# A transformer block on one core: the first transfers of x and of V's weights dealt anew between the two queues

## The chip, the core and the metric

The kernel runs on one core of one Trainium2 chip. The metric is device microseconds per execution: 555.67 us as the median of three runs (555.06 to 555.78).

## The reference, cut to what matters

One input x of 2048 rows by 576 columns (bfloat16) is normalised, then goes through a sliding-window attention and through a gated feed-forward, and the three are added.

```python
xn = _layernorm(x)                          # 2048 x 576, eps 1e-5
qkv = xn @ wqkv                             # 576 -> 3 * 576, 32 heads of 18
scores = einsum("bhqd,bhkd->bhqk", q, k) * 18 ** -0.5
scores = where(0 <= i - j < 256, scores, -1e9)
o = softmax(scores) @ v                     # heads joined again
attention = o @ wo                          # 576 -> 576
h = silu(xn @ w1) * (xn @ w3)               # 576 -> 4608
out = x + attention + h @ w2                # 4608 -> 576
```

## The kernel before, in words

The 2048 rows are worked in four chunks of 512 rows (`CH`), each of four tiles of 128 rows (`TB`). A chunk consists of the normalisation of its tiles, the projections to q, k and V, 36 units of the feed-forward's first half (`unit_pairs`, line 768, with the attention's steps dealt in between), and then the second half together with the output projection (`p2_mm`, line 839). The text speaks of tiles 1 to 4 of x as the change does; in the code they are t = 0 to 3.

Everything is written as a list of operations in program order (`add`). Each operation names the buffers that it reads (`r`), writes (`w`) or joins in writing (`j`), and `resolve` puts in the waits on semaphores. Every engine works through its own part of the list strictly in that order. So the order of lines is the order on each engine and on each of the two DMA queues, that of SyncE (q1 in the profile) and that of ScalarE (q10).

The change lies in the head, in what happens before the first feed-forward unit of the first chunk:

- SyncE requests tile 1 of x (`load_x`, line 306), V's weights for the contraction rows 0 to 511 in one transfer of 576 KB (line 897, buffer `wv`, key `wv`), the last 64 contraction rows in two small transfers (line 901, key `wvd`), and then the weights of q and k into the buffer `pt`: two transfers for the first half of the columns (line 927, key `wqk0`), two for the last 64 rows (line 931, key `wqkd`), two for the second half (`wqk1`). After these come the feed-forward weights (line 330), the first of which wait for tile 2's transposed values.
- ScalarE requests tiles 2, 3 and 4 of x and then loads its activation table (line 896).
- The normalisation of tile 1 is done by VectorE statistics (lines 396 and 399), a square root on ScalarE (line 369), a reciprocal (line 374) and the scaling (line 414). Tile 2's statistics are done on ScalarE (lines 387 and 390), those of tiles 3 and 4 on VectorE again. TensorE turns each tile (line 429), ScalarE copies the turned values to `xnT` (lines 442 and 448).
- V's projection (`proj_part`, line 500, kind "v") is done in two parts for each tile. In part 0 rows 0 to 63 of `wv` meet the first half of the columns and rows 64 to 127 the second half; in part 1 it is crossed. Each part therefore needs two quarters of `wv`. Part 1 ends with the 64 rows of `wvd`. The order on TensorE is: part 0 of tile 1, turning of tile 2, part 1 of tile 1, part 0 of tile 2, turning of tile 3, and so on.
- GpSimd regroups the weights of q and k from `pt` to `wp` (`deal`, line 952, eight copies, and one more copy on VectorE); the first of them needs `wqk0` and `wqkd`. The first part of q's projection (line 500, out of `xnT` and `wp`) needs the first two copies on GpSimd and the one on VectorE.
- `xn_swap` (line 463) then copies the halves of `xnT` crosswise to `xnS` by two transfers, behind the first six of the feed-forward weights. The first feed-forward unit reads `xnS` in its second half.

Of the kernel before, what the change touches and what calls it, by code (L numbers as in the profile page):

```python
# [44 lines left out]
class _Prog:  # L45
# [13 lines left out]
    def add(self, eng, fn, r=(), w=(), j=(), dma=None, after=()):  # L59
        deps = []  # L60
        for k in r:
            deps += self.bufs[k].writers
        for k in w:
            g = self.bufs.get(k)
            if g is not None:
                deps += g.ahead(eng)
        for k in j:
            g = self.bufs[k].before
            if g is not None:
                deps += g.ahead(eng)  # L70
        op = _Op(eng, fn, deps + list(after), dma)
        op.after = tuple(after)
        self.n[eng] += 1
        op.pos = self.n[eng]
        if dma is not None:
            self.dma_count[dma] = self.dma_count.get(dma, 0) + 16
            op.cnt = self.dma_count[dma]
        for k in r:
            self.bufs[k].readers.append(op)
        for k in w:  # L80
            self.bufs[k] = _Gen([op], self.bufs.get(k))
        for k in j:
            self.bufs[k].writers.append(op)
        for k in w:
            if self.bufs[k].before is not None:
                self.bufs[k].before.before = None
        self.ops.append(op)
        return op
# [76 lines left out]
def bass_parallel_sum__sliding_block__glu_gated_swiglu__prompt_kernel(  # L165
# [11 lines left out]
    D = A_x.shape[2]  # L177
# [11 lines left out]
    HD = D // 2  # L189
# [6 lines left out]
    add = P.add  # L196

    with ExitStack() as es:
# [17 lines left out]
        xnT = sb("xnT", [128, 2, 5, CH])  # L216
        xnS = sb("xnS", [128, 4, CH])
        wv = sb("wv", [128, 5, D])
# [83 lines left out]
        def load_x(t, eng="sp"):  # L302
            nonlocal xp_ctr
            s = xp_ctr % NXP
            xp_ctr += 1
            add(eng, lambda e: e.dma_start(xp[s][:], x2[t * 128:(t + 1) * 128, :]), w=[("xp", s)], dma=f"xp{s}")
            return s
# [167 lines left out]
        def proj_part(c, what, banks, part, behind=()):  # L475

            kind, i = what
            last = []
            early = kind == "v" and c == 0
            order = range(4 + part if kind == "v" else 5 - part)  # L480
            for n in order:
                for r in range(2):
                    x = r ^ part
                    kd, r0 = (4 if n == 4 else n), 64 * r
                    rows = slice(r0, r0 + 64)
                    out_ = PS[:, banks[x], :]
                    if kind == "q":
                        t = pair_of(c, i)[x]
                        st, mv = wp[rows, kd, t, :], xnT[rows, c % 2, kd, :]
                        keys = [("wp", t)] + xk(c)  # L490
                    elif kind == "8":
                        out_ = PS[:, banks[x], 0:CH // 2]
                        st, mv = wp[rows, kd, i, :], xnT[rows, c % 2, kd, x * (CH // 2):(x + 1) * (CH // 2)]
                        keys = [("wp", i)] + xk(c)
                    else:
                        out_ = PS[:, banks[x], 0:HD]
                        st, mv = xnT[rows, c % 2, kd, i * 128:(i + 1) * 128], wv[rows, kd, x * HD:(x + 1) * HD]
                        keys = ["wvd" if kd == 4 else "wv", (("xnTb" if kd // 2 else "xnTa"), i) if early and kd < 4 else ("xnT", c % 2, i)]
                    first = part == 0 and n == 0
                    op = add("pe", lambda e, out_=out_, st=st, mv=mv, n=n, r0=r0, first=first: e.matmul(  # L500
                        out_, st, mv, start=first, stop=(part == 1 and n == order[-1]), tile_position=(r0, 0)),
                        r=keys, after=behind if n == 0 else (), **{"w" if first else "j": [("ps", banks[x])]})
                    if n == order[-1]:
                        last.append(op)
            return last
# [384 lines left out]
                    p2_mm(ACC[half][tt] if turn is None or turn >= 0 else ACC[0][turn + 2], half, r, *args)  # L890


        xslot = {}
        for t in range(TB):
            xslot[t] = load_x(t, "act" if t else "sp")
        add("act", lambda e: e.preload_act_table_set("sqrt_and_others"))
        add("sp", lambda e: e.dma_start(
            wv[:, 0:4, :], A_wqkv[0:512, 2 * D:3 * D].rearrange("(kd p) f -> p kd f", p=128)),
            w=["wv"], dma="wv")
        for p in range(2):  # L900
            add("sp", lambda e, p=p: e.dma_start(
                wv[64 * p:64 * p + 64, 4, (1 - p) * HD:(2 - p) * HD],
# [21 lines left out]
        for h in range(2):  # L924
            for n in range(2):
# [3 lines left out]
                    dma=f"wqk{h}", **{"j" if n else "w": [f"wqk{h}"]})  # L929
# [119 lines left out]
        for c in range(NC):  # L1049
# [21 lines left out]
            early = [("h", n) for n in range(4 if c == 0 else 0, NHP)]  # L1071
# [111 lines left out]
            for u in range(NF):  # L1183
# [31 lines left out]
                if u in stat:  # L1215
                    t = (c + 1) * TB + stat[u]
# [4 lines left out]
                if u in apply:  # L1221
                    t = (c + 1) * TB + apply[u]
# [5 lines left out]
                if c == 0 and u == 13:  # L1228
                    for t in range(4):
# [24 lines left out]
            for item in p2_list(c):  # L1254
# [14 lines left out]
                elif n in (100, 120) and c + 2 < NC:  # L1269
                    t = (c + 2) * TB + (n == 120)  # L1270
# [34 lines left out]
```

## Time and profile before

| what | value |
|---|---|
| median of three runs | 555.67 us (555.06 to 555.78) |
| the profiled execution's own time | 555.25 us |
| its span, first to last instruction | 553.5 us |
| TensorE (PE) busy | 549.7 us, 99% of the span |
| VectorE / ScalarE / GpSimd busy | 57% / 47% / 38% |
| granted TensorE clock, mean | 1.000 |
| DMA queue of SyncE (q1) | 89138 packets, 62.80 MB |
| DMA queue of ScalarE (q10) | 38820 packets, 22.02 MB |

The profile comes from one execution, so sums are made against its own 555.25 us. The 1.75 us between it and the span lie around the program. The median of the runs is 0.42 us above the profiled execution. Times inside the trace are microseconds from the first instruction. A row of the timeline gives start, duration, engine, line, operation, names and count, and in brackets how long the engine was idle before it and what ended that. A row of the DMA issues gives the count, the size in KB (of 1024 bytes) and the time from issue to landing.

### The profile page before, as it was taken

How to read it: one execution, taken by the hardware profiler on the slowest of the kernel's cores; microseconds unless marked ns; L12 is line 12 of the kernel's file. 1: busy time of each engine (PE TensorE's matmuls, PEld its weight loads, DVE VectorE, ACT ScalarE, POOL GpSimd, SP SyncE). 2: the span in 40 equal slices, each digit the busy share in tenths (PEclk: the TensorE clock that was granted, in tenths of full speed). 3: DMA queues.
4: the chain of work that ended last, by engine and by line, in shares of the span. 5: the costliest groups of instructions: out<-in, count | busy, mean ns of one | idle time of the engine just before them, and what ended most of it. 6: DMA issues, size and time to landing. Idle time of an engine off the chain costs nothing.

```text
span 553.5 us, 18356 instructions
## 1 busy us (share of the span) xinstructions
PE 549.7 (99%) x8072; PEld 338.6 (61%) x8072; DVE 313.3 (57%) x587; ACT 259.3 (47%) x365; POOL 210.8 (38%) x380
## 2 busy tenths in 40 slices
PE   8999999999999999999999999999999999999998
PEld 5677544777555544477765454557776545445776
DVE  7476797710468886651056988655105567866311
ACT  7457776000288567700037857760005784775000
POOL 4324675400047456530005745643001553663100
DMA  9997799476577953756746885466673773541750
GB/s 246 204 199 173 199 202 229 129 202 181 141 144 145 188 134 92 186 141 194 185 111 140 173 157 146 124 143 164 183 181 85 139 172 102 152 117 44 194 151 23
DMA packets 128038, 86.00 MB, mean 155 GB/s; under 512 B 35702, under 2 KB 125646, under 8 KB 127958
## 3 DMA queue, kind: packets, MB, share of 16 engines
q1 hardware_dynamic: 89138, 62.80, 49.9%
q10 hardware_dynamic: 38820, 22.02, 15.7%
q8 instruction: 63, 1.03, 0.8%
q14 instruction: 17, 0.14, 0.1%
HBM read 71.29 MB, written 2.36 MB: 133 GB/s over the span
## 4 chain that ended last, share of the span: by engine, by line
PE 99%; DMA 1%; DVE 0%; issue 0%; ACT 0%
PE ps L768 51%; PE ps L839 29%; PE ps L500 10%; PE ps L630 6%; PE ps L698 3%; DMA xp<-in_A_x_dram 1%; PE ps L429 0%; DVE stats L396 0%; DVE xn L414 0%; ACT sd L369 0%; DVE ofin L861 0%; PE ps L915 0%; DVE mv L399 0%; DVE rstd L374 0%
## 5 line engine op out<-in xcount | busy, mean ns | idle before, releaser
L768 PE MATMUL ps<-xnT,w 64*128 64x512 bf16 x1400 | 186.4, 376 | 0.0
L768 PE MATMUL ps<-xnS,w 64*128 64x512 bf16 x1120 | 152.4, 376 | 0.0
L839 PE MATMUL ps<-w,hT 64*128 64x288 bf16 x2292 | 143.7, 282 | 0.0
L783 DVE SCALAR_TENSOR_TENSOR gs<-th,ps 128x512 bf16<-128x512 bf16 x144 | 97.9, 680 | 78.8 <-ACT th L777 78.0
L839 PEld LDWEIGHTS ps<-w,hT 64*128 64x128 bf16 x2292 | 112.3, 94 | 29.5 <-issue 0.2
L777 ACT ACTIVATE th<-ps 128x512 bf16<-128x512 f32 x144 | 85.6, 594 | 60.6 <-PE ps L768 59.7
L768 PEld LDWEIGHTS ps<-xnT,w 64*128 64x128 bf16 x1400 | 69.8, 94 | 61.6
L786 DVE SCALAR_TENSOR_TENSOR hT<-gs,ps 128x512 bf16<-128x512 bf16 x144 | 98.9, 687 | 5.0
L667 POOL TENSOR_TENSOR pt<-pt,mk 128x256 bf16<-128x256 bf16 (+1 forms) x143 | 85.6, 623 | 25.7 <-ACT pt L639 25.7
L639 ACT ACTIVATE pt<-ps 128x1024 bf16<-128x1024 f32 (+1 forms) x80 | 80.8, 1010 | 24.6 <-PE ps L630 24.1
L667 POOL TENSOR_TENSOR hT<-hT,mk 128x256 bf16<-128x256 bf16 (+1 forms) x52 | 30.3, 604 | 160.5 <-ACT hT L639 160.5
L768 PEld LDWEIGHTS ps<-xnS,w 64*128 64x128 bf16 x1120 | 55.6, 94 | 49.0
L513 ACT ACTIVATE stage<-ps 128x512 bf16<-128x512 f32 x16 | 9.6, 597 | 139.4 <-PE ps L500 139.4
L870 DVE TENSOR_TENSOR ofin<-ps,xp 128x288 bf16<-128x288 f32 x31 | 12.2, 451 | 98.5 <-PE ps L839 98.5
L630 PE MATMUL ps<-qv,kv 64*128 64x320 bf16 (+4 forms) x528 | 51.9, 260 | 0.0
L630 PEld LDWEIGHTS ps<-qv,kv 64*128 64x128 bf16 x528 | 26.8, 94 | 28.1 <-ACT pt L639 1.7
L500 PE MATMUL ps<-xnT,wp 64*128 64x512 bf16 (+1 forms) x360 | 38.4, 355 | 0.0
L731 DVE STREAM_TRANSPOSE od<-oq 128x256 bf16<-128x256 bf16 x64 | 25.4, 425 | 12.1 <-POOL oq L724 12.1
L639 ACT ACTIVATE hT<-ps 128x1024 bf16<-128x1024 f32 (+1 forms) x28 | 28.4, 1015 | 7.6 <-PE ps L630 7.4
L667 POOL TENSOR_TENSOR stage<-stage,mk 128x256 bf16<-128x256 bf16 (+1 forms) x44 | 24.8, 586 | 14.2 <-ACT stage L639 14.2
L639 ACT ACTIVATE stage<-ps 128x1024 bf16<-128x1024 f32 (+1 forms) x24 | 24.3, 1014 | 6.9 <-PE ps L630 6.8
L500 PEld LDWEIGHTS ps<-xnT,wp 64*128 64x128 bf16 x360 | 18.3, 94 | 14.5 <-ACT stage L513 0.2
(94 smaller groups left out, 395.9 us busy)
## 6 DMA issues: line engine op xcount, KB each, us to landing
w<-in_B_w_dram SPq DMA_DIRECT2D x210, 192.0 KB, 4.2
w<-in_B_w_dram ACTq DMA_DIRECT2D x70, 288.0 KB, 3.6
xp<-in_A_x_dram SPq DMA_DIRECT2D x29, 144.0 KB, 4.2
out_dram<-ofin SPq DMA_DIRECT2D x31, 72.0 KB, 1.7
xnS<-xnT SPq DMA_DIRECT2D x8, 256.0 KB, 4.7
oT<-od SPq DMA_DIRECT2D x56, 36.0 KB
pt<-in_A_wqkv_dram SPq DMA_DIRECT2D x4, 288.0 KB, 5.3
hT<-in_B_w_dram SPq DMA_DIRECT2D x6, 192.0 KB, 7.4
```

Of the source, the lines that this page charges most:

```text
L500: op = add("pe", lambda e, out_=out_, st=st, mv=mv, n=n, r0=r0, first=first: e.matmul(out_, st, mv, start=first, stop=(part == 1 and n == ...
L630: add("pe", lambda e, r0=r0, out_=out_, kb=kb, q0=q0, nb=nb: e.matmul(out_, kb4[r0:r0 + 64, g, kb + NV - NB, :] if kb < 0 else kv[r0:r0 + ...
L639: add("act", lambda e: e.activation(pt_slot(sl)[:, :, 0:w], PS[:, SC[0]:SC[1] + 1, 0:w], ACT.Exp, scale=scale), r=[("ps", b) for b in SC], ...
L667: add("pool", lambda e, vb=vb, mm=mm: e.tensor_tensor(vb, vb, mm, ALU.mult), r=(key if n == 0 else []) + ["mk"], **{"w" if n == 0 else "j" ...
L698: add("pe", lambda e, p=p, q=q, pr=pr, sl=sl, g=g, pos=pos, q0=q0, nb=nb, col=col, first=first, n=n: e.matmul(PS[32 * q:32 * q + VW, banks ...
L731: add("dve", lambda e: e.transpose(od[i][:, g % 2, c0:c0 + CH // 2], oq[:, c0:c0 + CH // 2]), r=["oq", "oq0"], **{"j" if half or g % 2 els ...
L768: op = add("pe", lambda e, n=n, r0=r0, r=r, k=k, src=src: e.matmul(PS[:, b0 + r, :], wt[r0:r0 + 64, k, fl * 128:(fl + 1) * 128], src, star ...
L777: add("act", lambda e: e.activation(th[i][:], PS[:, bg, :], ACT.Tanh, scale=0.5), r=[("ps", bg)], w=[("th", i)])
L783: add("dve", lambda e: e.scalar_tensor_tensor(out=gs[i][:], in0=th[i][:], scalar=1.0, in1=PS[:, bg, :], op0=ALU.add, op1=ALU.mult), r=[("t ...
L786: add("dve", lambda e: e.scalar_tensor_tensor(out=hT[:, u, :], in0=gs[i][:], scalar=0.5, in1=PS[:, bu, :], op0=ALU.mult, op1=ALU.mult), r= ...
L839: op = add("pe", lambda e: e.matmul(PS[:, bank, 0:w], stat, move, start=new, stop=False, skip_group_check=True, **tile), r=keys, after=hel ...
L870: add("dve", lambda e: e.tensor_tensor(ofin[:, o, :], PS[:, bank, 0:HD], xp[xs[n]][:, d0:d0 + HD], ALU.add), r=[("ps", bank), ("xp", xs[n] ...
```

## The change

V's weights for the rows 0 to 511 are requested in four quarters of 144 KB, each of 64 partitions, instead of in one transfer of 576 KB. The two quarters that part 0 multiplies (key `wv0`) are requested by ScalarE, behind tile 2 of x and ahead of its table load. The two that part 1 multiplies (key `wv1`) are requested by SyncE, behind tiles 1, 3 and 4 of x. ScalarE's list so holds three transfers ahead of the table load as before, with other contents. SyncE's holds three more than before ahead of `wvd`. V's matmuls wait for the key of their own part.

```diff
-                        keys = ["wvd" if kd == 4 else "wv", ...
+                        keys = ["wvd" if kd == 4 else f"wv{part}", ...
...
+        def load_wv(part, eng):
+            for p in range(2):
+                x = p ^ part
+                add(eng, lambda e, p=p, x=x: e.dma_start(
+                    wv[64 * p:64 * p + 64, 0:4, x * HD:(x + 1) * HD],
+                    A_wqkv[0:512, 2 * D + x * HD:2 * D + (x + 1) * HD].rearrange("(kd q p) f -> q p kd f", q=2, p=64)[p, :, :, :]),
+                    dma=f"wv{part}", **{"j" if p else "w": [f"wv{part}"]})
+
         xslot = {}
         for t in range(TB):
-            xslot[t] = load_x(t, "act" if t else "sp")
+            xslot[t] = load_x(t, "act" if t == 1 else "sp")
+        load_wv(0, "act")
         add("act", lambda e: e.preload_act_table_set("sqrt_and_others"))
-        add("sp", lambda e: e.dma_start(
-            wv[:, 0:4, :], A_wqkv[0:512, 2 * D:3 * D].rearrange("(kd p) f -> p kd f", p=128)),
-            w=["wv"], dma="wv")
+        load_wv(1, "sp")
```

More of the change, by code (lines that the diff above doesn't have):

```diff
@@ L497, in proj_part @@
                         st, mv = xnT[rows, c % 2, kd, i * 128:(i + 1) * 128], wv[rows, kd, x * HD:(x + 1) * HD]
-                        keys = ["wvd" if kd == 4 else "wv", (("xnTb" if kd // 2 else "xnTa"), i) if early and kd < 4 else ("xnT", c % 2, i)]
+                        keys = ["wvd" if kd == 4 else f"wv{part}", (("xnTb" if kd // 2 else "xnTa"), i) if early and kd < 4 else ("xnT", c % 2, i)]
                     first = part == 0 and n == 0
```

## The prediction, made before the changed kernel was run

> **What bounds the kernel now.** I read the page first: the busy time of the engines (part 1) and the chain that ended last (part 4).
>
> ```profile
> PE 549.7 (99%) x8072; PEld 338.6 (61%) x8072; DVE 313.3 (57%) x587; ACT 259.3 (47%) x365; POOL 210.8 (38%) x380
> ...
> PE 99%; DMA 1%; DVE 0%; issue 0%; ACT 0%
> ```
>
> TensorE is busy in 99% of the span, and the chain lies on it. The changed transfers all land in the first microseconds, so they can matter only as far as they shift the moment from which TensorE never waits again. The chain of waits for the first 24 us shows where that moment is (start, duration, what).
>
> ```profile
> 0.79 2.78 DMA xp<-in_A_x_dram
> 3.60 0.83 DVE stats L396 x2
> ...
> 4.69 0.30 ACT sd L369
> ...
> 5.22 0.42 DVE xn L414
> ...
> 6.49 0.67 PE ps L500 x8
> 7.16 0.21 PE ps L429 x10
> ...
> 10.46 10.64 PE ps L500 x118
> ```
>
> The head runs from tile 1's landing (0.79 + 2.78 = 3.57) over its normalisation to V's first part at 6.49. From 10.46 on TensorE feeds itself. V's weights do not appear in this chain, and of x only tile 1. So the question is not what the kernel gains when V's weights or tiles 3 and 4 come sooner, but whether a transfer that is hidden now comes out of its cover. For that I read the timeline, first the issues and ScalarE's start.
>
> ```profile
> 0.80 1.44 ACTq L306 DMA_DIRECT2D xp<-in_A_x_dram  x3
> 1.25 0.42 SPq L897 DMA_DIRECT2D wv<-in_A_wqkv_dram  x1
> 1.71 1.20 SPq L901 DMA_DIRECT2D wv<-in_A_wqkv_dram  x2
> 1.72 0.52 ACTq L306 DMA_DIRECT2D xp<-in_A_x_dram  x1
> 2.27 1.28 ACT L896 ACT_TABLE_LOAD   x1 [2.27 <-issue]
> 3.77 0.69 ACT L387 ACTIVATE hT<-xp 128x576 f32<-128x576 bf16 x1 [0.22 <-DMA xp<-in_A_x_dram]
> 4.69 0.60 SPq L931 DMA_DIRECT2D pt<-in_A_wqkv_dram  x1
> 5.33 1.14 SPq L927 DMA_DIRECT2D pt<-in_A_wqkv_dram  x2
> 8.25 4.90 SPq L330 DMA_DIRECT2D w<-in_B_w_dram  x6
> 13.84 0.60 SPq L463 DMA_DIRECT2D xnS<-xnT  x1
> ```
>
> Then those who use what is loaded, from the same view.
>
> ```profile
> 5.75 0.45 DVE L396 BATCH_NORM_STATS2 stats<-xp 128x6 f32<-128x288 bf16 x1
> 5.98 0.37 ACT L442 ACTIVATE xnT<-ps 128x256 bf16<-128x256 bf16 x1
> 7.21 0.48 PEld L500 LDWEIGHTS ps<-wv,xnT 64*128 64x128 bf16 x10
> 7.26 0.77 DVE L396 BATCH_NORM_STATS2 stats<-xp 128x6 f32<-128x288 bf16 x2
> 7.38 0.29 ACT L369 ACTIVATE sd<-mv,eps 128x1 f32<-128x1 f32 x1 [0.33 <-DVE mv L399]
> 8.00 0.11 PEld L500 LDWEIGHTS ps<-wv,xnT 64*128 64x128 bf16 x4 [0.30 <-ACT xnT L442]
> 10.13 0.84 POOL L952 COPY wp<-pt 128x360 f32<-128x360 f32 x2 [6.14 <-DMA pt<-in_A_wqkv_dram]
> 10.75 0.23 DVE L952 COPY wp<-pt 128x45 f32<-128x45 f32 x1
> 11.48 0.79 PEld L500 LDWEIGHTS ps<-xnT,wp 64*128 64x128 bf16 x10
> 21.52 0.81 PEld L768 LDWEIGHTS ps<-xnS,w 64*128 64x128 bf16 x8
> ```
>
> And the DMA issues, each asked for the moment of one issue, with the time from issue to landing. In this order: V's weights, tile 4 of x (the third on ScalarE's queue), the second of the small `wvd`, the second `wqkd`, the second half of `xnS`.
>
> ```profile
> wv<-in_A_wqkv_dram SPq DMA_DIRECT2D x1, 576.0 KB, 4.5
> ...
> xp<-in_A_x_dram ACTq DMA_DIRECT2D x1, 144.0 KB, 4.6
> ...
> wv<-in_A_wqkv_dram SPq DMA_DIRECT2D x1, 36.0 KB, 4.4
> ...
> pt<-in_A_wqkv_dram SPq DMA_DIRECT2D x1, 144.0 KB, 5.3
> ...
> xnS<-xnT SPq DMA_DIRECT2D x1, 256.0 KB, 6.8
> ```
>
> What is hidden, and by how much: V's weights land at 1.25 + 4.5 = 5.75, and V's first part also needs ScalarE's copy, which ends at 5.98 + 0.37 = 6.35: 0.60 us of cover. `wqkd` lands at 4.69 + 5.3 = 9.99 and GpSimd, idle for 6.14 us until then, starts its copies at 10.13. The two that q's first part needs end at 10.97, VectorE's at 10.98, and TensorE comes to q at 11.48: about 0.5 us of cover. The second half of `xnS` lands at 13.84 + 6.8 = 20.64 and is read at 21.52: 0.88 us. The shortest cover that lies behind all of the changed transfers is that of `wqkd`.
>
> How fast the transfers go is told by the windows (stretch, busy time by engine, clock, DMA share, GB/s).
>
> ```profile
> 4.00:5.00 1.00, 0.95 (x23) 0.65 (x19) 0.62 (x3) 0.86 (x4) 0.00 (x0) 1.00 1.09 389
> 6.00:7.40 1.40, 1.29 (x30) 0.96 (x30) 1.33 (x6) 1.06 (x6) 0.00 (x0) 1.00 1.15 312
> 8.00:8.50 0.50, 0.50 (x10) 0.23 (x8) 0.50 (x5) 0.41 (x2) 0.00 (x0) 1.00 0.92 161
> 11.50:16.00 4.50, 4.50 (x50) 2.61 (x48) 2.90 (x6) 2.91 (x7) 4.13 (x11) 1.00 1.13 221
> ```
>
> The share is about 1 in all four, so the DMA engines are the limit here, and not the issues. By the order of the queues the first stretch holds x and V's weights (128 partitions, pieces of 1152 bytes), the second the first half of the q and k weights (128 partitions, 576 bytes), the third `wqkd` (64 partitions, 2304 bytes), the fourth the feed-forward weights (64 partitions, 1024 bytes). Transfers to 64 partitions go at 161 to 221 GB/s, those to 128 at 312 to 389. The granted clock is 1.00 throughout.
>
> **The change part by part.**
>
> *Tiles 3 and 4 of x sooner.* VectorE takes up tile 3 at 5.75 and tile 4 at 7.26 with no wait for a transfer in the row, straight behind other work. Their earlier landing is worth nothing. Tile 1 stays the first on its queue and tile 2 on its own, beside the same neighbours; tile 1's landing would go into the sum one to one. I take 0, with bounds of 0.2 us either way: tile 2, first on the other queue, is taken up at 3.77 and tile 1 at 3.60.
>
> *ScalarE's list.* It issues three transfers as before. A quarter of V's weights has the shape nearest to `wvd` and `wqkd`, which cost 1.20 / 2 = 0.60 us an issue against 0.52 for tile 4. So the table load moves from 2.27 to about 0.80 + 0.41 + 2 x 0.64 = 2.5 and ends at 3.8. Line 387 starts at 3.77 because tile 2 lands then: at most some 0.05 us late. It is done by 4.6, before the square root of tile 1 at 4.69. Cost 0; if that cover of about 0.1 us is gone, the chain is late by the rest.
>
> *SyncE's list.* Two tiles of x (0.46 and 0.52 by ScalarE's rows) and one more issue for `wv1` (2 x 0.62 - 0.46) put everything behind about 1.75 us later: the second `wqkd` goes out at 6.4 instead of 4.69, the last `wqk1` ends at 5.33 + 1.14 + 1.75 = 8.2, and the feed-forward weights at 8.25 wait for tile 2's copy anyway. As transfers wait 4.4 to 5.3 us from issue to landing in a full queue, mostly behind others, later issues do not starve it. Cost 0.
>
> *V's first part on the ACT queue.* Its second quarter has the place that tile 4 has now, third on ScalarE's queue. That landed at 1.72 + 4.6 = 6.32, against the 6.35 of the copy. From below: 5.75, where V's weights land now, no wait. From above: 6.32 plus half of the 1.15 us extra worked out next, 6.9, a wait of 0.55. Behind this wait stand on TensorE the turning of tile 2, part 1 and all that follows. But the turned tile 2 is there at 7.37 and ScalarE first does the square root of tile 3, at 7.38 to 7.67, which waits for VectorE. So about 0.2 to 0.3 us of lateness costs nothing. I take a landing of 6.5, and 0.
>
> *The rate of V's 589,824 bytes.* At 389 GB/s they take 1.52 us. In pieces of 576 bytes over all partitions (312) they would take 1.89: 0.37 more. At the rate of the feed-forward weights (221) 2.67: 1.15 more. At that of `wqkd` (161) 3.66: 2.15 more. Half of the bytes (`wv0`) travel beside x tiles or beside the opposite half on the other queue, and half (`wv1`) mostly alone, first one half of the partitions and then the other. So I take the mean of the first two, 0.76. All that stands behind on SyncE's queue lands 0.76 later.
>
> [...]
>
> *Part 1.* `wvd` landed at about 2.33 + 4.4 = 6.73 as the last of the same bytes; 0.76 later is 7.49, and `wv1`, ahead of its 73,728 bytes (0.24 us at 312), 7.25. Part 1 starts at 7.21 and comes to `wvd` some 0.4 us later. Behind it TensorE waits 0.30 us for ScalarE at 8.00, which covers 0.04 us of lateness. Cost 0.
>
> *q's first part.* `wqkd` lands at 9.99 + 0.76 = 10.75, so GpSimd's two copies end at 11.73 and VectorE's at 11.0 to 11.1. TensorE, at q since 11.48, waits 0.25 us. From below 0 (0.37 stays under the cover of 0.5), from above 0.65 (1.15) or 1.65 (2.15). This wait and one in V do not add: who is late in V comes to q later.
>
> *Behind it.* `xnS` lands up to 0.76 later, within its 0.88, and TensorE comes 0.25 later itself. Cost 0.
>
> **Sum.** 555.25 + 0.25 = 555.50 for the profiled execution; the median is 0.42 above it: 555.92, say 555.9 us. 0.2% of 555.67 is 1.1 us, about what a measurement of this kernel can tell from no change.
>
> **The rivals.**
>
> *All hidden.* The quarters go at 312 GB/s because the two queues fill both halves of the partitions; `wqkd` lands at 10.36 and TensorE does not notice. For it: x beside them spreads over all partitions. Against: `wv1` is alone on its queue at the end. 555.7 us, within 0.2%.
>
> [...]
>
> *Slower by a slow `wqkd`.* The weights of q and k come out so late that GpSimd holds TensorE for longer than 1.1 us. It decides from 0.5 + 1.1 = 1.6 us of extra, which is V's weights below 188 GB/s. At the 161 of the third window q waits 1.65: 557.3 us. For it: `wqkd` reads the same matrix as V's weights, to 64 partitions too. Against: that is half a microsecond, in which two transfers change over.
>
> *Faster.* Tile 1 lands sooner because no 576 KB transfer starts behind it. It is worth 0.2 us by the bound above, 555.5; for 1.1 us the landing would have to be at 2.5, and nothing in the rows speaks for that.
>
> **How the numbers follow.** Forecast 0.60, all hidden 0.15, halves one after the other 0.11, slower 0.09, faster with the bound of 0.2 us or by what I do not see 0.05. The first two and the third in most runs lie within 1.1 us. Slower by over 0.2%: 0.09 and a third of the 0.11, with a little for the unnamed: 0.14. Faster by over 0.2%: 0.04. Same: 0.82. The range goes from 555.1, tile 1 sooner with the scatter of the runs (555.06 to 555.78), to 557.0, which takes in the halves one after the other (556.3, or 556.7 with that scatter) and leaves out the upper half of the slower case.
>
> **What would show it.** In the profile after: line 387 at 3.75 to 3.85; V's first part at 6.4 to 6.6; GpSimd's first copy at 10.5 to 11.3 instead of 10.13; the weight load of q's first part behind an idle time ended by GpSimd, at 11.6 to 12.1; a lower rate at 5 to 7 us; the distance from there to the end unchanged. I am wrong if line 387 or tile 1 moves by more than 0.2 us, if V's first part starts after 6.8, or if TensorE waits for `xnS` or a feed-forward weight at 20 to 40 us.

## The result: 0.33% slower, outside the range

| | median of 19 runs | ratio to before, 95% interval |
|---|---|---|
| before | 555.54 us | |
| changed | 557.52 us | 1.0033 (1.0021 to 1.0044) |
| changed, a second series (first experiment) | 556.93 us against 555.48 | 1.0023 (1.0013 to 1.0033) |

Predicted were 555.9 us, 555.1 to 557.0, and no difference that can be measured. The kernel became slower by 1.3 to 1.8 us.

The execution of the changed kernel that was profiled in the first series had a granted TensorE clock of 0.65 from 4.9 us on (0.656 on average) and took 827.17 us, so it is not in the ratio and its trace is not read for times. The same kernel was profiled again in the first experiment, at a clock of 1.000, and every row "of the changed kernel" below is from that execution: 556.28 us, with a span of 554.5 us against 553.5 before. It is one of the shorter executions of its series, so its rows can explain 1.0 us of the loss. What the others have beyond that no trace here shows; two of the other ten had a granted clock of 0.997 on average, of which the last section tells.

The page, span and part 1, tells little. TensorE still takes 99%.

```profile
span 554.5 us, 18359 instructions
...
PE 550.2 (99%) x8071; PEld 332.4 (60%) x8072; DVE 313.2 (56%) x587; ACT 259.2 (47%) x365; POOL 211.2 (38%) x380
```

The chain of waits over the first 24 us (start, duration, what) has changed its kind. Before, it ran over tile 1 and its normalisation. Now it runs over ScalarE's second issue and the 5.10 us of a quarter of V's weights, which lands at 7.15.

```profile
1.24 0.78 ACTq L896
...
2.05 5.10 DMA wv<-in_A_wqkv_dram
...
7.19 0.66 PE ps L500 x8
...
10.86 10.95 PE ps L500 x114
```

V's first part starts at 7.19 instead of 6.49. The timeline of the changed kernel shows ScalarE's start and SyncE's issues of the second `wqkd` and of `wqk1`, at 6.72 and 7.99.

```profile
2.05 0.64 ACTq L896 DMA_DIRECT2D wv<-in_A_wqkv_dram  x1
2.72 1.28 ACT L905 ACT_TABLE_LOAD   x1 [2.72 <-issue]
4.01 0.68 ACT L387 ACTIVATE hT<-xp 128x576 f32<-128x576 bf16 x1
6.72 0.60 SPq L938 DMA_DIRECT2D pt<-in_A_wqkv_dram  x1
7.99 0.51 SPq L934 DMA_DIRECT2D pt<-in_A_wqkv_dram  x1
```

Its DMA issues give the time of the second `wqkd` and of the second `wqk1` from issue to landing. They land at about 10.96 and 14.25, where before it was 9.99 and 11.98.

```profile
pt<-in_A_wqkv_dram SPq DMA_DIRECT2D x1, 144.0 KB, 4.2
pt<-in_A_wqkv_dram SPq DMA_DIRECT2D x1, 288.0 KB, 6.3
```

Those who use what is loaded, from the timeline of the changed kernel (the bracket is the idle time before, and what ended it):

```profile
7.19 0.36 PEld L500 LDWEIGHTS ps<-wv,xnT 64*128 64x128 bf16 x8 [1.05 <-DMA wv<-in_A_wqkv_dram]
11.10 1.87 POOL L959 COPY wp<-pt 128x360 f32<-128x360 f32 x5 [7.09 <-DMA pt<-in_A_wqkv_dram]
12.00 0.79 PEld L500 LDWEIGHTS ps<-xnT,wp 64*128 64x128 bf16 x10 [0.26 <-issue]
14.30 1.66 POOL L959 COPY wp<-pt 128x180 f32<-128x180 f32 x3 [1.34 <-DMA pt<-in_A_wqkv_dram]
16.01 2.06 PEld L500 LDWEIGHTS ps<-xnT,wp 64*128 64x128 bf16 x22 [0.46 <-POOL wp L959]
22.19 0.95 PEld L768 LDWEIGHTS ps<-xnS,w 64*128 64x128 bf16 x8
```

In the kernel before, GpSimd made its eight copies in one go:

```profile
10.13 3.55 POOL L952 COPY wp<-pt 128x360 f32<-128x360 f32 x8 [6.14 <-DMA pt<-in_A_wqkv_dram]
```

Three covers in a row are gone, and each one takes over from the one before. Set against the same instruction before, TensorE is late by 0.70 us at V's first part and by 0.39 at V's last tile (10.77 against 10.38), because its wait for ScalarE's copies has absorbed the rest. It is late by 0.52 at q's first part, because GpSimd got `wqkd` late: its first copies began at 11.10 instead of 10.13. (That TensorE waited for them there is worked out; the row names no releaser.) Behind q's third part it is late by about 0.8, between 0.67 and 0.87 by single weight loads. There GpSimd's copies come in two groups now: for the last three it was idle for 1.34 us until `wqk1` had landed, and TensorE waited 0.46 us for them. At the first feed-forward unit's reads of `xnS` the lateness is 0.67 (22.19 against 21.52), at the end about 1.0. What arises behind that point isn't read: the spans of three traces of the kernel before also differ by up to 0.7 us (553.5 to 554.2).

The windows (stretch, busy time by engine, clock, DMA share, GB/s) tell when the transfers fell behind. First the kernel before, then the changed one:

```profile
3.50:4.50 1.00, 1.00 (x33) 1.00 (x30) 0.87 (x3) 0.78 (x3) 0.49 (x1) 1.00 1.08 381
4.50:5.50 1.00, 0.61 (x8) 0.15 (x4) 0.60 (x3) 0.86 (x3) 0.00 (x0) 1.00 1.08 383
```

```profile
3.50:4.50 1.00, 1.00 (x23) 1.00 (x21) 0.94 (x3) 0.99 (x2) 0.50 (x1) 1.00 0.78 182
4.50:5.50 1.00, 0.80 (x16) 0.52 (x14) 0.54 (x3) 1.00 (x4) 0.00 (x0) 1.00 1.02 303
```

In one microsecond 199 KB fewer than before (381 - 182) were moved, at a DMA share of 0.78 instead of 1.08, and in the next 80 fewer (383 - 303). At the 381 GB/s of before that is about 0.7 us of transfers, the larger part of the 0.97 by which `wqkd` lands late. The trace of the first series has this stretch too, before its clock fell: 209 GB/s from 3.5 to 4.5.

### The profile page after: what moved, and what is told of

The parts are those of the page before. It is cut to its first block, busy times and chain, and to the rows that moved or that the text cites. A ratio compares the mean times of both kernels' runs of the same rounds, so it can differ in the third digit from the quotient of the medians.

```text
span 825.4 us, 18360 instructions
## 1 busy us (share of the span) xinstructions
PE 821.2 (99%) x8072; PEld 413.9 (50%) x8072; DVE 315.6 (38%) x587; ACT 264.1 (32%) x365; POOL 212.2 (26%) x380
## 4 chain that ended last, share of the span: by engine, by line
PE 99%; DMA 1%; ACTq 0%; DVE 0%; issue 0%
PE ps L768 51%; PE ps L839 29%; PE ps L500 10%; PE ps L630 6%; PE ps L698 3%; DMA wv<-in_A_wqkv_dram 1%; ACTq L896 0%; PE ps L429 0%; ACTq L306 0%; DVE ofin L861 0%
## 5 line engine op out<-in xcount | busy, mean ns | idle before, releaser
L768 PE MATMUL ps<-xnT,w 64*128 64x512 bf16 x1400 | 267.4, 509 | 0.0
L768 PE MATMUL ps<-xnS,w 64*128 64x512 bf16 x1120 | 217.4, 509 | 0.0
L839 PE MATMUL ps<-w,hT 64*128 64x288 bf16 x2292 | 214.5, 365 | 0.0
L839 PEld LDWEIGHTS ps<-w,hT 64*128 64x128 bf16 x2292 | 138.8, 117 | 73.6 <-issue 1.1
L768 PEld LDWEIGHTS ps<-xnT,w 64*128 64x128 bf16 x1400 | 83.3, 117 | 113.2 <-issue 104.4
L768 PEld LDWEIGHTS ps<-xnS,w 64*128 64x128 bf16 x1120 | 66.7, 118 | 89.6 <-issue 85.8
L630 PE MATMUL ps<-qv,kv 64*128 64x320 bf16 (+4 forms) x528 | 67.4, 329 | 0.0
L630 PEld LDWEIGHTS ps<-qv,kv 64*128 64x128 bf16 x528 | 32.5, 118 | 48.3 <-issue 39.9
L500 PE MATMUL ps<-xnT,wp 64*128 64x512 bf16 (+1 forms) x360 | 56.7, 476 | 0.0
L500 PE MATMUL ps<-wv,xnT 64*128 64x288 bf16 x288 | 29.9, 363 | 1.0 <-DMA wv<-in_A_wqkv_dram 1.0
```

What stands on the lines that cost most here:

```text
L630: add("pe", lambda e, r0=r0, out_=out_, kb=kb, q0=q0, nb=nb: e.matmul(out_, kb4[r0:r0 + 64, g, kb + NV - NB, :] if kb < 0 else kv[r0:r0 + ...
L768: op = add("pe", lambda e, n=n, r0=r0, r=r, k=k, src=src: e.matmul(PS[:, b0 + r, :], wt[r0:r0 + 64, k, fl * 128:(fl + 1) * 128], src, star ...
L839: op = add("pe", lambda e: e.matmul(PS[:, bank, 0:w], stat, move, start=new, stop=False, skip_group_check=True, **tile), r=keys, after=hel ...
```

## The experiments

In the table, "partitions" is the number that each transfer of V's weights for the rows 0 to 511 writes, "landed" the last of these and of `wqkd` in the trace, and the next two columns the GB/s of two windows. The ratio is to the kernel before on the same chip. The last column counts the executions whose mean granted clock was 0.997 or 0.994 instead of 1.000; of the kernel before, none of 104 was.

| kernel | partitions | ratio (95%) | landed `wv`, `wqkd` | 3.5 to 4.5 | 5.5 to 6.5 | clock lower |
|---|---|---|---|---|---|---|
| before | 128 | | 5.78, 9.99 | 381 | 319 | 0 of 104 |
| e1 the change | 64 | 1.0023 (1.0013 to 1.0033) | 7.63, 10.96 | 182 | 298 | 2 of 11 |
| e2 x alone | 128 | 1.0042 (1.0025 to 1.0059) | 8.40, 11.97 | 136 | 319 | 6 of 11 |
| e3 quarters alone | 64 | 1.0038 (1.0024 to 1.0051) | 7.61, 10.98 | 185 | 246 | 1 of 12 |
| e4 halves by columns | 128 | 1.0030 (1.0016 to 1.0044) | 6.30, 11.98 | 361 | 242 | 0 of 11 |
| e5 V's first weights first | 64 | 1.0045 (1.0029 to 1.0062) | 8.36, 11.54 | 175 | 256 | 1 of 7 |
| e6 V whole, then x | 128 | 1.0021 (1.0009 to 1.0033) | 5.44, 10.86 | 381 | 198 | 1 of 10 |
| e7 x alone, filled | 128 | 1.0095 (1.0076 to 1.0114) | 10.16, 11.50 | 358 | 323 | 4 of 4 |
| e8 columns, filled | 128 | 1.0030 (1.0015 to 1.0045) | 7.93, 10.66 | 361 | 347 | 3 of 10 |
| e9 V whole on ScalarE | 128 | 0.9997 (0.9986 to 1.0007) | 6.71, 10.28 | 370 | 349 | 0 of 12 |
| e10 the same, in two | 128 | 1.0001 (0.9992 to 1.0010) | 7.12, 10.72 | 354 | 352 | 0 of 10 |
| e11 the same, in two | 64 | 1.0057 (1.0042 to 1.0071) | 8.29, 11.78 | 211 | 297 | 8 of 10 |
| e12 one on each queue | 128 | 1.0015 (1.0003 to 1.0027) | 5.35, 10.25 | 387 | 191 | 0 of 10 |
| e13 one on each queue | 64 | 1.0039 (1.0024 to 1.0054) | 7.61, 12.30 | 238 | 243 | 2 of 7 |

**The change again (e1).**

> The changed kernel once more, for a trace at the full clock (the trace at hand ran at a granted clock of 0.66) and for the size of the loss on the same chip as the next three. Theory S (quarters to 64 partitions are slow, so V's and q's weights land late): 1.5 to 2.0 us slower than before; V's first part starts about 7.4 instead of 6.49 and GpSimd's first copy at 11.5 to 11.8 instead of 10.13. Theory C (the lost time belongs to the lower clock and not to the transfers): V's first part starts by 6.7, GpSimd's first copy by 10.8, the loss under 0.6 us.

1.0023 (1.0013 to 1.0033), 1.3 us, with the rows shown above. The loss is there again, at a clock of 1.000, so Theory C is out; every size is somewhat below those of Theory S.

**The dealing of x alone (e2).** V's weights stay one transfer over 128 partitions on SyncE's queue, behind three tiles of x instead of one.

```diff
-            xslot[t] = load_x(t, "act" if t else "sp")
+            xslot[t] = load_x(t, "act" if t == 1 else "sp")
```

> Only the tiles of x are dealt as in the change; V's weights stay one transfer of 128 partitions on SyncE's queue, now behind three tiles of x, and ScalarE requests tile 2 alone. Theory S (the quarters cost): within 0.4 us of before, the q and k weights land at 10.0 to 10.3; V's weights land 0.8 us later (295 KB of x at 389 GB/s are in front of them), at 6.5, so V's first part starts at 6.6. Theory O (the place behind x costs, whoever carries the weights): 1 us or more slower, V's first part at 7.2 or later.

It is slower by 0.42%, though V's transfer for the rows 0 to 511 is to 128 partitions: Theory O. (Six of its eleven executions had a lower clock; the median of the other five, 556.77 us, is 0.23% above 555.48.) Windows and timeline of this kernel:

```profile
3.50:4.50 1.00, 1.00 (x33) 0.95 (x30) 0.97 (x3) 0.78 (x2) 0.50 (x1) 1.00 0.79 136
4.50:5.50 1.00, 0.30 (x4) 0.11 (x2) 0.60 (x4) 0.93 (x3) 0.00 (x0) 1.00 0.89 166
```

```profile
8.45 0.36 PEld L500 LDWEIGHTS ps<-wv,xnT 64*128 64x128 bf16 x8 [2.42 <-DMA wv<-in_A_wqkv_dram]
```

For two microseconds the transfers go at 136 and 166 GB/s, and TensorE stands for 2.42 us before V. Moving x is not free, as I had put it.

**The quarters alone (e3).** Tiles 2 to 4 of x stay on ScalarE's queue, and all four quarters go on SyncE's. The edit is against the changed kernel.

```diff
-            xslot[t] = load_x(t, "act" if t == 1 else "sp")
-        load_wv(0, "act")
+            xslot[t] = load_x(t, "act" if t else "sp")
+        load_wv(0, "sp")
...
         load_wv(1, "sp")
```

> Only the split: the tiles of x as before, V's weights as four quarters of 64 partitions, all on SyncE's queue behind tile 1, those of part 0 first. Theory S: V's first part does not wait (its two quarters land by 6.0), but the q and k weights land 1.0 to 1.6 us later, GpSimd's first copy at 11.1 to 11.8, 0.6 to 1.2 us slower than before. Theory O: the split alone costs nothing, GpSimd's first copy by 10.5, within 0.3 us of before.

It is slower by 0.38%. So either part of the change costs, alone, about as much as both together, and the two do not add. Here V waits for its weights for 0.62 us only, where Theory S had no wait. Most of the loss comes later, at q's third part, behind GpSimd's wait for `wqk1`, which neither theory names:

```profile
15.03 1.65 POOL L959 COPY wp<-pt 128x180 f32<-128x180 f32 x3 [2.04 <-DMA pt<-in_A_wqkv_dram]
16.74 0.33 PEld L500 LDWEIGHTS ps<-xnT,wp 64*128 64x128 bf16 x6 [1.17 <-POOL wp L959]
```

**Halves by columns (e4).** The change with the same places in the queues, but each half of V's weights one transfer to all 128 partitions; a matmul waits for the key of its columns.

```diff
         def load_wv(part, eng):
-            for p in range(2):
-                x = p ^ part
-                ...
+            add(eng, lambda e: e.dma_start(
+                wv[:, 0:4, part * HD:(part + 1) * HD],
+                A_wqkv[0:512, 2 * D + part * HD:2 * D + (part + 1) * HD].rearrange("(kd p) f -> p kd f", p=128)),
+                dma=f"wv{part}", w=[f"wv{part}"])
```

> As the change in place, queue, bytes and piece size, but V's weights are halved by columns, so each half goes to 128 partitions in one transfer; V's first part needs both halves. Theory S: the q and k weights land at 10.2 to 10.5 (0.37 us for the smaller pieces), GpSimd's first copy at most at 10.6; V's first part waits for the second half, until about 6.9; at most 0.6 us slower than before. Theory O: as slow as the change, GpSimd's first copy at 11.5 or later.

The slow stretch at 3.5 is gone (361 GB/s) and V starts at 6.40. But another stands at 5.5, and `wqkd` comes to GpSimd at 12.12:

```profile
5.50:6.50 1.00, 0.75 (x18) 0.51 (x20) 0.96 (x5) 0.97 (x6) 0.00 (x0) 1.00 0.98 242
```

```profile
12.12 1.86 POOL L957 COPY wp<-pt 128x360 f32<-128x360 f32 x5 [8.13 <-DMA pt<-in_A_wqkv_dram]
13.02 0.79 PEld L500 LDWEIGHTS ps<-xnT,wp 64*128 64x128 bf16 x10 [1.73 <-DVE wp L957]
```

That is Theory S for V's weights and Theory O for those of q. So the 64 partitions are not needed for a loss, and V in time is not enough to avoid one.

**The kernel before, twice, and x alone once more.** One trace each, to tell whether the slow stretches belong to single executions.

> The kernel before, unchanged, for a second trace of its head. Theory R (the low DMA rate of 3.4 to 4.6 us in the traces of the changed kernel is a stall of single executions, and the kernel before merely has the cover for it): the rate falls under 250 GB/s for at least 0.8 us somewhere between 3 and 6 us here too, and some landing moves by over 0.7 us. Theory D (the stall comes with the new dealing): V's weights land at 5.6 to 6.0, the second of the last 64 rows for q and k at 9.8 to 10.3, no such stretch.

> The kernel before once more: a third trace of its head, with the same two expectations as for the second.

> Tiles of x dealt as in the change, V's weights in one transfer: a second trace. Theory D: V's weights land at 8.0 to 8.8 again (8.40 in the first trace), the rate is under 250 GB/s for 1.5 us or more after 3.4. Theory R: they land by 7.2, the stretch is elsewhere or missing.

The windows of the first and the second trace of the kernel before, and of the second of x alone:

```profile
3.50:4.50 1.00, 1.00 (x33) 1.00 (x30) 0.91 (x3) 0.81 (x3) 0.50 (x1) 1.00 1.04 361
```

```profile
3.50:4.50 1.00, 1.00 (x23) 1.00 (x21) 0.83 (x3) 0.72 (x3) 0.49 (x1) 1.00 1.07 380
```

```profile
3.50:4.50 1.00, 1.00 (x23) 1.00 (x21) 0.97 (x3) 0.78 (x2) 0.49 (x1) 1.00 0.76 111
```

Three of three traces of the kernel before have no such stretch, and two of two of x alone have it (with landings of V's weights at 8.40 and 7.71). It belongs to the order of the transfers. Chance executions are out.

**V's first weights first (e5).** The change, with the two quarters of `wv0` right behind the first tile on each queue.

```diff
             xslot[t] = load_x(t, "act" if t == 1 else "sp")
+            if t == 1:
+                load_wv(0, "act", (0,))
+                load_wv(0, "sp", (1,))
-        load_wv(0, "act")
```

> The change, but the two quarters that V's first part multiplies go out directly behind the first tile of each queue, one on each. Theory V (the wait of V's first part sets the loss): V's first part at 6.5, at most 0.5 us slower than before. Theory Q (the weights of q and k set the end, whatever V does): V's first part at 6.5, yet GpSimd's first copy at 10.9 to 11.3 and the loss 0.8 to 1.4 us, as with the change.

1.0045 (1.0029 to 1.0062): no better than the change. Timeline of this kernel:

```profile
6.95 0.36 PEld L500 LDWEIGHTS ps<-wv,xnT 64*128 64x128 bf16 x8 [0.46 <-DMA wv<-in_A_wqkv_dram]
8.41 0.97 PEld L500 LDWEIGHTS ps<-wv,xnT 64*128 64x128 bf16 x18 [0.45 <-DMA wv<-in_A_wqkv_dram]
16.05 1.07 POOL L961 COPY wp<-pt 128x180 f32<-128x180 f32 x2 [2.51 <-DMA pt<-in_A_wqkv_dram]
```

V's first part waits less than in the changed kernel (0.46 against 1.05 us), and the loss is no smaller: part 1 waits too now, and GpSimd waits 2.51 us for `wqk1`. That V's wait alone sets the loss (Theory V) is refuted; the loss is also above the 0.8 to 1.4 us of Theory Q, at 2.5 us.

**V whole, then tiles 3 and 4, on SyncE's queue (e6).** This asks whether it is enough to keep V's transfer whole and early.

```diff
-            xslot[t] = load_x(t, "act" if t else "sp")
+            xslot[t] = load_x(t, "act" if t == 1 else "sp")
+            if t == 1:
+                add("sp", lambda e: e.dma_start(wv[:, 0:4, :], ...   # as before, moved up
```

> The kernel before, but tiles 3 and 4 of x go out on SyncE's queue behind V's one transfer, so that ScalarE's queue holds tile 2 alone and runs dry at about 3.2 us. Theory B (the rate holds only while both queues have work): a stretch under 250 GB/s begins at 3.3 to 3.6, V's weights land at 6.8 or later, over 0.8 us slower than before. Theory X (the stretch comes with x tiles ahead of V's weights on SyncE's queue): no such stretch, V's weights land by 5.6, and tile 3 (at 6.2) delays VectorE by some 0.4 us: 0 to 0.5 us slower.

1.0021 (1.0009 to 1.0033). Windows and timeline of this kernel:

```profile
3.50:4.50 1.00, 1.00 (x23) 1.00 (x21) 0.91 (x3) 0.75 (x2) 0.49 (x1) 1.00 1.08 381
...
5.50:6.50 1.00, 0.92 (x18) 0.47 (x16) 0.89 (x5) 0.95 (x5) 0.00 (x0) 1.00 0.93 198
```

```profile
11.00 1.86 POOL L953 COPY wp<-pt 128x360 f32<-128x360 f32 x5 [7.01 <-DMA pt<-in_A_wqkv_dram]
```

ScalarE's queue has nothing left after tile 2, and yet the rate holds at 381 while V's long transfer runs alone on SyncE's queue. So the theory that the rate holds only while both queues have work is refuted in that form. The stretch comes behind that transfer, where the tiles and the small weights follow it. Theory X, with at most 0.5 us, missed it too: the loss is 1.2 us.

**x alone, with the first half of q's and k's weights on ScalarE's queue (e7); and the same filling for the halves by columns (e8).** What ScalarE requests here, SyncE no longer does.

```diff
+        load_qk(0, 0, "act")
+        load_qk(0, 1, "act")        # the second kernel: only the first of these
         add("act", lambda e: e.preload_act_table_set("sqrt_and_others"))
```

> Tiles of x dealt as in the change, V's weights in one transfer on SyncE's queue, and the first half of the weights of q and k requested by ScalarE behind tile 2, so that both queues have work until about 6 us. Theory B: no stretch under 250 GB/s from 3.4 to 5.5, in which the traces without this had 46 to 202; V's weights land by 7.2 although they share the engines with 576 KB more. Theory X: the stretch stays, V's weights land at 8 or later.

> V's weights halved by columns over 128 partitions at the places of the change, and one of the two transfers of the first half of q's and k's weights moved to ScalarE's queue behind them. Theory B: the slow stretch that began at 5.5 (222 to 314 GB/s, when ScalarE's queue had run dry at 4.5) goes or moves behind 6; GpSimd's first copy at 10.0 to 11.0 instead of about 12.1, at most 0.6 us slower than before. Theory X: the stretch stays, GpSimd's first copy after 11.5, 1.2 us or more slower.

The first is slower by 0.95% (1.0076 to 1.0114), with a lowered clock in all four executions. The rate stays at 358, 296 and 323 GB/s over the three windows from 3.5, but V's weights now share it with 576 KB more, land at 10.16, and TensorE waits for them (waits by line: us in total, times, longest):

```profile
PE ps L500 <- DMA wv<-in_A_wqkv_dram: 3.9, 1, 3.9
```

The second is at 1.0030 (1.0015 to 1.0045), as without the filling: the stretch at 5.5 is gone (347 instead of 242), and V waits 1.3 us instead. So Theory B is right about the stretch in both and wrong about the time. In these two, what was put on the second queue and is needed later took its share from what is needed first.

**V's weights whole on ScalarE's queue (e9).** x is dealt as in the change; V's one transfer stands where the change has `wv0`.

```diff
-            xslot[t] = load_x(t, "act" if t else "sp")
+            xslot[t] = load_x(t, "act" if t == 1 else "sp")
...
-        add("sp", lambda e: e.dma_start(wv[:, 0:4, :], ...
+        add("act", lambda e: e.dma_start(wv[:, 0:4, :], ...    # ahead of the table load
```

> The change without its split: tiles 1, 3 and 4 of x on SyncE's queue, tile 2 and V's weights, in one transfer of 128 partitions, on ScalarE's. Theory B: both queues have 128-partition work until about 5.3, the rate stays over 330 GB/s from 2.5 to 5, V's weights land at 5.6 to 6.3, V's first part at 6.5, within 0.4 us of before. Theory X: under 250 GB/s at 3.4 to 4.6 as with the change, over 0.8 us slower.

0.9997 (0.9986 to 1.0007). Windows and timeline of this kernel:

```profile
3.50:4.50 1.00, 1.00 (x23) 1.00 (x21) 0.92 (x3) 0.77 (x2) 0.51 (x1) 1.00 1.08 370
...
5.50:6.50 1.00, 0.69 (x16) 0.41 (x16) 0.96 (x5) 0.97 (x6) 0.00 (x0) 1.00 1.12 349
```

```profile
10.41 3.58 POOL L952 COPY wp<-pt 128x360 f32<-128x360 f32 x8 [6.41 <-DMA pt<-in_A_wqkv_dram]
```

No slow stretch, and GpSimd's eight copies run without a gap. The dealing of x costs nothing if V's weights go whole on the other queue. Against x alone, only the place of one transfer differs, and the window at 3.5 goes at 370 instead of 136. But that place is another queue and also an earlier one: V's transfer is requested at 1.24 us, ahead of the requests for tiles 3 and 4 at 1.25 and 1.71, and in x alone at 2.18, behind them. Here V's weights land 1.0 and 1.7 us sooner than in the two traces of x alone, of which 0.94 us is the earlier request, and in the window the rates are 370 against 136 and 111. Whether the queue or the order does it, the pair does not tell.

**Two transfers of 288 KB, to 128 (e10) or to 64 partitions (e11), on one queue.** These settle what the halves themselves do. Both are the kernel just shown with V's weights cut in two; the rows of 1152 bytes, their number, the queue and the key are the same.

```diff
+ wv[:, 2*n:2*n+2, :]         # half of the contraction rows, 128 partitions
+ wv[64*p:64*p+64, 0:4, :]    # all of them, 64 partitions
```

> As the kernel with V's weights in one transfer on ScalarE's queue, but in two transfers of 288 KB, each 128 partitions and half of the contraction rows (pieces of 1152 bytes as there). Theory P (what slows the transfers of the change is that they go to 64 partitions): no slow stretch, V's weights land by 6.9, within 0.4 us of before. Theory T (more and shorter transfers slow them): under 250 GB/s for 0.5 us or more in 3.4 to 5.5, V's weights land at 7.2 or later, 0.5 us or more slower.

> The same two transfers of 288 KB on ScalarE's queue with pieces of 1152 bytes, but each to 64 partitions with all of the contraction rows. Theory P: a stretch under 250 GB/s from about 3.5, V's weights land at 7.3 or later (589,824 bytes at 221 GB/s are 1.15 us longer than at 389), over 0.6 us slower than before and at least 0.4 us behind the kernel with the same count of transfers to 128 partitions. Theory T: the same as that kernel, within 0.3 us.

1.0001 (0.9992 to 1.0010) against 1.0057 (1.0042 to 1.0071). Windows and timeline of the one with 128 partitions, then of the one with 64:

```profile
3.50:4.50 1.00, 1.00 (x27) 1.00 (x25) 0.81 (x2) 0.66 (x3) 0.49 (x1) 1.00 1.11 354
```

```profile
7.16 0.36 PEld L500 LDWEIGHTS ps<-wv,xnT 64*128 64x128 bf16 x8 [0.92 <-DMA wv<-in_A_wqkv_dram]
```

```profile
3.50:4.50 1.00, 1.00 (x23) 1.00 (x21) 0.88 (x3) 0.99 (x2) 0.50 (x1) 1.00 0.89 211
```

```profile
8.34 0.61 PEld L500 LDWEIGHTS ps<-wv,xnT 64*128 64x128 bf16 x8 [2.18 <-DMA wv<-in_A_wqkv_dram]
```

The first starts V at 7.16, as late as the changed kernel does (7.19), and loses nothing that can be measured: what stands behind comes in time, and TensorE is late by 0.28 us at q and no more after it. The second goes at 211 GB/s instead of 354, which is 0.60 of it, and starts V at 8.34. (Its loss holds some of the clock too: the two of its ten executions at a clock of 1.000 took 557.23 and 557.24 us, 0.30% above the 555.59 of the kernel before, against 0.57% for all. At 3.5 to 4.5 us both have 1.00.)

The 0.60 holds for this window alone: in the next, from 4.5 to 5.5, the two kernels go at 296 and 297 GB/s. Why the transfers to 64 partitions go more slowly, the traces do not show.

**The same two, one on each queue at the same time (e12, e13).** Each stands directly behind the first tile of its queue, with tiles 3 and 4 behind on SyncE's.

```diff
             xslot[t] = load_x(t, "act" if t == 1 else "sp")
+            if t == 1:
+                load_wv(0, "act")
+                load_wv(1, "sp")
```

> V's weights in two transfers of 288 KB to 128 partitions, each half of the contraction rows, one directly behind the first tile of each queue; tiles 3 and 4 of x behind them on SyncE's. Theory P: over 330 GB/s until 5, V's weights land by 5.6, V's first part at 6.5; later stretches as in the trace with V's one transfer ahead of these tiles on SyncE's queue, 0.3 to 1.2 us slower than before. Theory T: under 250 GB/s from 3.2 on.

> The same places and bytes, but each of the two transfers goes to 64 partitions, the two halves side by side on the two queues. Theory P, halves do not add up: under 250 GB/s from 3.0 to 4.5 (127 to 222 in the trace with two quarters side by side), V's weights land 0.8 us or more later than with the 128-partition pair, and the tiles of x behind them late. If the two halves add up: over 330 GB/s as with the 128-partition pair, V's weights land within 0.3 us of it.

1.0015 (1.0003 to 1.0027) with 128 partitions, 1.0039 (1.0024 to 1.0054) with 64. Windows of the first, then of the second:

```profile
3.50:4.50 1.00, 1.00 (x26) 1.00 (x24) 0.88 (x3) 0.73 (x2) 0.49 (x1) 1.00 1.09 387
...
5.50:6.50 1.00, 0.71 (x18) 0.46 (x20) 0.96 (x5) 0.97 (x6) 0.00 (x0) 1.00 0.81 191
```

```profile
3.50:4.50 1.00, 1.00 (x26) 1.00 (x24) 0.82 (x3) 0.67 (x2) 0.50 (x1) 1.00 0.91 238
```

Opposite halves side by side on two queues go at 238 GB/s, 13% above the 211 of one after the other and far from the 387 of the pair to 128 partitions.

**What the experiments leave.** Shown: with the number of partitions as the only difference, transfers to 64 of them cost 0.56% on one queue (1.0057 against 1.0001), about half of it by the clock that falls in the wait (by the two executions at full clock), and quarters alone make the kernel before slower by 0.38%. On two queues the difference is 0.24% (1.0039 against 1.0015), but the two intervals touch, and without the two executions at a lower clock it is 0.13%. Shown too: x dealt as in the change costs nothing with V's weights on ScalarE's queue and 0.42% with them behind the tiles on SyncE's (0.23% at a clock of 1.000). Open: what makes the other slow stretches, for which no transfer of `wv` to 64 partitions but the small `wvd` is needed. As the halves by columns lose 0.30% at the very places of the change, it is open too how much of the change's own loss is due to the 64 partitions. In x alone a stretch stands at 3.5 to 5.5, with tiles of x and then V's one transfer on SyncE's queue and nothing on ScalarE's. It is not that the DMA engines lacked requests there. The rows of the queues from 3.5 to 5.5 (packets, MB, share of 16 engines), in the kernel before and then in x alone:

```profile
q1 hardware_dynamic: 462, 0.50, 70.9%
q10 hardware_dynamic: 248, 0.26, 36.9%
```

```profile
q1 hardware_dynamic: 285, 0.30, 84.4%
```

At 84% of the engines' time only 285 packets were moved, against 710 at 108% (the share sums the packets' own times, and passes 100% where these overlap): a packet took 95 ns on average instead of 49. What held them, the trace does not show. In the halves by columns (242), V then x (198) and one on each queue (191) a stretch stands at 5.5, where SyncE's queue passes to the small weights in rows of 576 bytes, and ScalarE's last transfer has landed (at 4.93, 3.72 and 5.00). The same passage goes at 319 to 352 in the kernel before and with V's weights whole or in two on ScalarE's queue, whose last transfer lands at 6.32, 6.71 and 7.12. But the small weights are also requested earlier in these three (the first `wqk0` at 2.95 to 3.44 us, against 3.90 to 3.97). Which of the two it is, or the order itself, was not isolated.

## Why the prediction was wrong

**Tiles and ScalarE's list: right in cost.** VectorE took up tile 1 at 3.52 instead of 3.60. The first quarter took 0.78 us to issue instead of 0.64, so that the table load began at 2.72, not 2.5, and line 387 at 4.01. That is beyond the 3.85 that I had set as a bound, and 0.24 us later than before, one of the signs of being wrong. It ended at 4.69, and the square root of tile 1 started at 4.70, 0.01 later than before: no cost, but with nothing left of the cover.

**V's first part: the first step that failed.** I took the landing of tile 4 (6.32) as the place of the second quarter and 6.5 as its landing. It was 7.15, also above the 6.9 of my upper bound, and V started 0.70 late, at 7.19, past the 6.8 that I had named as a sign of being wrong. Tile 4 is to 128 partitions, and the quarter is not: with the halves by columns, to 128 partitions at the same places, ScalarE's landed at 4.93 and V started at 6.40. The absorption behind it was right: the 0.2 to 0.3 us of cover took 0.31 (0.70 to 0.39).

**The rate: mis-sized.** I took 0.76 us extra for all that stands behind V's weights, the mean of 0.37 and 1.15. `wqkd` landed 0.97 later. The argument for the lower end, that the quarters travel beside x tiles or beside the opposite half and so fill all partitions, is what the runs refute: 182 GB/s in the changed kernel beside a tile of x, and 238 for opposite halves. Part of the 0.97 may be the later request, which I had put at no cost: the second `wqkd` went out at 6.72 instead of 4.69. With one transfer of 128 partitions on each queue it went out 1.0 later and landed 0.26 later; no run shows 2.0 alone.

**q's first part: in its ranges.** GpSimd began at 11.10 (10.5 to 11.3 forecast), q at 12.00 (11.6 to 12.1). I gave 0.25 for it, and it is 0.52, of which 0.39 had been there since V. That V's wait and q's do not add was right.

**What I left out: `wqk1`.** I called the cover of `wqkd` the shortest behind the changed transfers and stopped there. The second `wqk1` landed 2.3 us later than before, GpSimd ran out of work for 1.34 us and q's third part took TensorE from 0.52 to about 0.8. Of the 2.3 us, 0.97 is the lateness of `wqkd`, which goes ahead of it; what makes the other 1.3 was not isolated. Before, GpSimd's last copy ended at 13.68 (10.13 + 3.55) and q's third part began at about 15. This third cover, of over 1 us, appears in no step of the prediction, and in the kernel with the quarters alone its end brings the lateness from 0.5 to about 1.5.

**Behind it: right.** `xnS` and the feed-forward weights cost nothing: the lateness is no larger at the first unit (0.67) than behind q's third part.

So the sum of 0.25 was about 0.7 at the first feed-forward unit and 1.0 over the span. Of the rivals, "halves one after the other", with its 556.3 us, is the nearest: at the 221 GB/s of the feed-forward weights, 1.15 us extra, `wqkd` lands at 9.99 + 1.15 = 11.14 (10.96 measured) and q waits 0.65 us (late by 0.52), which makes 555.25 + 0.65 + 0.42. That is still below the 557.5: it leaves out `wqk1`, and the median lies further above the traced execution (0.65 us in its series) than the 0.42 that the sum took. "Slower by a slow `wqkd`" has the nearer time, 557.3, but by luck: it needs `wqkd` at about 12.1. I had rows with the rates in hand, 221 and 161 GB/s to 64 partitions against 312 to 389 to 128, and gave the halves one after the other a chance of 0.11, on the argument of mixed neighbours; no row of the kernel before showed two opposite halves side by side.

## What to carry to other kernels

In a head, list every consumer of every transfer that stands behind the moved one, each with its cover: when one cover breaks the next shortest decides, and here the third did. A transfer that has to be split is split along the contraction rows, over all 128 partitions, as that cost nothing here (1.0001), where halves of the partitions cost 0.57%, the clock included. Here it was best to request what is needed first whole and early on the second queue; filling that queue with what is needed later cost 0.95%, the clock included. No version here was faster than the kernel before (the best is at 0.9997): its transfers were under cover already.

## What the runs showed of the hardware that was not expected

**The granted clock fell behind a short wait of TensorE in four traces, for 3.4 us in three of them and for longer in the fourth.** In the kernel with two transfers to 64 partitions on ScalarE's queue TensorE stood for 2.18 us before V, and then the windows of that kernel have a clock (third value from the end) of one half:

```profile
7.00:8.00 1.00, 0.00 (x0) 0.00 (x0) 0.96 (x5) 0.36 (x2) 0.00 (x0) 0.96 1.16 233
8.00:9.00 1.00, 0.66 (x6) 0.42 (x8) 0.79 (x5) 0.00 (x0) 0.00 (x0) 0.50 1.16 312
...
11.00:12.00 1.00, 1.00 (x22) 0.77 (x20) 0.95 (x4) 0.12 (x1) 0.08 (x1) 0.83 1.05 263
```

From 0.96 and 0.83 in the outer windows, with one half between them, the time at half clock is 0.08 + 3 + 0.34 = 3.4 us. The same sum gives 3.4 us in the one with 64 partitions on each queue (0.82 at 7, 0.97 at 11), after a wait of 1.46 us (waits are counted at the weight loads), and in the halves by columns with the filling (0.57 at 8, 0.72 at 11), after one of 1.47. In x alone with the filling, after 4.16 us, it was longer: 0.91 at 7 and one half in all six windows from 8 to 14, so 6.2 us at least. So part of the loss of these four kernels is the clock and not the transfers. Nor does it fall every time: the traced execution of x alone kept its clock at 1.00 after a wait of 2.42 us, but 6 of its 11 executions had a mean of 0.997, the mean that goes with 3.4 us at half clock in the trace above. Among the kernels whose longest wait is the one before V, the executions with a lower clock become more as the traced wait becomes longer, with one exception: 0 of 12 (0.65 us), 0 of 10 (0.92), 2 of 11 (1.05, the change), 2 of 7 (1.46), 3 of 10 (1.47), 8 of 10 (2.18), 6 of 11 (2.42), 4 of 4 (4.16). What sets the 3.4 us, and which executions keep their clock, no trace here shows.

**Issue time by shape.** On ScalarE, the two issues of 288 KB of V's weights each took 0.45 and 0.49 us to 128 partitions (e10), and 0.78 and 0.66 to 64 (e11).
